# Four plain weight pairs instead of two, and column halves in turn for the products of values and scores, in a kernel of decayed attention and two feed-forward networks

## The chip, the cores and the metric

The kernel runs on one core of one Trainium2 chip. The metric is the device time of one execution in microseconds, here the median of three runs. Five engines matter: PE (TensorE, the matmuls; its weight loads are listed apart as PEld), DVE (VectorE), ACT (ScalarE), POOL (GpSimd) and SP, which here issues the DMAs. Each works its own instructions in the order in which they were written.

## The reference, cut to what matters

The input is q, k, v of shape (2, 8, 768, 64): 2 sequences, 8 heads, 768 tokens, 64 channels.

```python
# attention with decay lam (one number per head), in blocks of 64 tokens
intra = (qb @ kb.T) * Dmask          # Dmask[i, j] = lam ** (i - j) for i >= j, else 0
out   = intra @ vb + (qb * lam_pow) @ kv_state
kv_state = lam ** 64 * kv_state + (kb * rev_pow).T @ vb
# two feed-forward networks, one after the other, on 1536 tokens x 512 channels
h = x @ w_in                         # 512 -> 2048
x = (h * tanh(log1p(exp(h)))) @ w_out            # 2048 -> 512, mish
h = x @ w_in2
y = (h * (1 / (1 + exp(-h)))) @ w_out2           # silu
```

All is in float32 and the result is float32.

## The kernel before, in words

Tokens are worked in chunks of 128 in the attention (12 chunks, 6 for each sequence) and in blocks of 512 in the networks (three blocks, t = 0, 1, 2). A network's 2048 hidden units are 16 tiles n of 128; the second network's tiles go on as n = 16 to 31. Tiles come in pairs p = n // 2, and in groups g of four tiles. NF is 16 and NG, the groups of a network, is 4; so the kernel has groups 0 to 7, and pairs 0 to 15.

**Numbers in two parts.** Matmuls of the networks run on fp32r operands. To keep float32's precision each operand is split into a high part, which ACT casts (xh, wh, gh), and a low part, the rest, which POOL or DVE subtracts (xl, wl, gl). A product is then three matmuls: high x high, low x high, high x low. The weights arrive by DMA in another form (their 64 bits are unpacked on DVE): `split_op` (L122 to L138) is five DVE operations for each half of a tile (half 0 is the part of w_in, half 1 that of w_out), and `run_parts` (L173) has ACT cast wh and POOL subtract wl (L178, L179). In the second network's first group ACT takes over the first of the five (L94) from an item on.

**Two ways to project.** A projection of one tile and one token block, `emit_h` (L407 to L423), is 12 matmuls. For the token blocks 0 and 1, most pairs of tiles are done together by `Block` (L528 on) in seven products of 6 matmuls (m1 to m7) instead of eight, by the scheme of Strassen and Winograd: that needs sums of quarters of x (`sums`, made once for each network by `make_sums` or `evac`), and differences of quarters of w (`sum_pair`, four DVE operations L164 for each pair, two casts, two subtractions). m1's bank "a" is copied to bank "b" by ACT (L568), m5's to `fifth` (L573), and DVE adds that to further banks (L557); m2 goes on adding into bank "a", so it waits for the copy. Pairs in `plain` have no `sum_pair`; they are projected with `emit_h`. Output products, `emit_o` (L425 to L445), are 12 matmuls into four banks `po`, which `evac` (L457) adds to the accumulators at the end of a group: DVE adds (L465), or in a network's group 0 ACT copies (L463). At the end of the first network `evac` also makes the next network's input from the accumulator: xh by ACT (L475), xl by POOL (L478) through the list `rest`, whose entries `run_rest` issues one or more at a time.

**Order.** The order of every engine's work is written by hand. First comes the attention of four chunks, then 12 steps, each with one chunk of attention (while there are any), one projection and one output product of group 0. Then come the groups 1 to 7, each a list of items; after each item `run_parts`, `run_rest`, `run_sums` (sums of x, a list at a time) and `run_split(k)` (k split operations) are called, and the loads of freed slots. Groups 1 and 4 (`first`) begin with four `emit_h` of their first pair in place of seven products, since the sums aren't made yet. The last two, or four, output products of block 2 of a group are the `fills` of the next. In groups 1 and 4 the second pair B (pairs 3 and 9) goes through seven products and the group's output products of t = 0 and 1 stand between B's products and the projections of t = 2.

**The attention's products.** `emit_S` makes the scores (K is 64, a product uses one half of the array's rows, the two heads of a pair in turn), `emit_state` the state (64 columns, the two heads of a pair in turn on the column halves), and `emit_O` (L338) the output of a chunk: four products on state (L344), then for each of eight heads the values times the masked scores (L350), 64 of the array's 128 columns each: all four pairs for the first column half, then all four for the second. DVE multiplies the scores by the mask (L307). Each float32 product shows as two records in the trace.

Of the kernel before, what the change touches and what calls it, by code (L numbers as in the profile page):

```python
# [7 lines left out]
F32 = mybir.dt.float32  # L8
# [9 lines left out]
def decay_attention_mish_silu_kernel(  # L18
# [8 lines left out]
    nc = tc.nc  # L27
    P = 128
# [5 lines left out]
    NP = H // 2  # L34
    T = 512
# [43 lines left out]
    parts = []  # L79

    pre = []
    plain = (2, NF // 2)
    silu = []
    uses = {}

# [252 lines left out]
    def emit_O(n):  # L338
        c = n % CPS
        vn = nat.pop(n)[3]  # L340
        px = ps_a.tile([P, NP, C], F32, tag="a", name="px")
        if c > 0:
            for p in range(NP):
                nc.tensor.matmul(  # L344
                    px[:, p, :], lhsT=states[n % 2][:, p, :], rhs=qd[n][:, p, :],
                    start=(p == 0), stop=False, skip_group_check=True,
                )
        for hh in range(2):
            for p in range(NP):
                nc.tensor.matmul(  # L350
                    px[64 * hh : 64 * hh + 64, p, :], lhsT=vn[:, 2 * p + hh, :], rhs=sm[n][:, hh, p, :],
                    start=(c == 0 and p == 0), stop=(p == NP - 1), skip_group_check=True,
                )
        xslots.append(held.pop(("x", n)))
        xh, xl = x_tile(n // CPB)
        o = slice((n % CPB) * C, (n % CPB + 1) * C)
        xf = wk.tile([P, T], F32, tag="wa", name="xf").rearrange("p (a c) -> p a c", a=NP)
        nc.scalar.copy(xf, px)
        nc.scalar.copy(xh[:, :, o], xf)  # L359

        def finish():
            (nc.vector if n < PH else nc.gpsimd).tensor_tensor(out=xl[:, :, o], in0=xf, in1=xh[:, :, o].bitcast(F32), op=ALU.subtract)

        return finish
# [82 lines left out]
    def cast(i, f):  # L447
        return lambda: nc.scalar.copy(sums[i][0], f)

    def low(i, f):  # L450
        hi, lo = sums[i]
        return lambda: nc.vector.tensor_tensor(out=lo, in0=f, in1=hi.bitcast(F32), op=ALU.subtract)  # L452

    def tt(out, in0, in1, op):
        return lambda: nc.vector.tensor_tensor(out=out, in0=in0, in1=in1, op=op)

    def evac(mm, g, t):  # L457
        if g == 0:
            accs[mm, t] = (accp if t == 0 else late[1]).tile([P, 4, T], F32, tag="acc", name="acc")
        acc = accs[mm, t]  # L460
        for j in range(4):
            if g == 0:
                nc.scalar.copy(acc[:, j, :], po[t][j])  # L463
            else:
                nc.vector.tensor_tensor(out=acc[:, j, :], in0=po[t][j], in1=acc[:, j, :], op=ALU.add)  # L465
            if g == NG - 1 and mm == 1:
                r0 = t * T + j * P
                nc.sync.dma_start(out[r0 : r0 + P, :], acc[:, j, :])
        if g < NG - 1 or mm == 1:
            return  # L470

        xh, xl = x_tile(t)

        def part(j):
            nc.scalar.copy(xh[:, j, :], acc[:, j, :])  # L475
            rest.append((
                (t, j),
                lambda: nc.gpsimd.tensor_tensor(  # L478
                    out=xl[:, j, :], in0=acc[:, j, :], in1=xh[:, j, :].bitcast(F32), op=ALU.subtract
                ),  # L480
            ))

        if t != 1:
            for j in range(4):
                part(j)
            return
        a1, a2 = accs[0, 0], acc

        f1 = late[0].tile([P, 2, T], F32, tag="t4", name="s1", bufs=1)
        f3, f4 = a2[:, 0:2], a1[:, 2:4]  # L490
        add, sub = ALU.add, ALU.subtract
        drain = lambda: run_rest(len(rest))
        summing.extend([
            [tt(f1, a2[:, 0:2], a2[:, 2:4], add)],
            [cast(0, f1), lambda: part(0), lambda: part(1)],
            [low(0, f1), lambda: part(2), lambda: part(3), tt(f1, f1, a1[:, 0:2], sub)],
            [drain, cast(1, f1), tt(f4, f4, f1, sub)],
            [low(1, f1), tt(f3, a1[:, 0:2], f3, sub)],
            [cast(2, f3)],
            [low(2, f3)],  # L500
        ])
        last_sum.append([cast(3, f4), low(3, f4)])
# [5 lines left out]
    def make_sums():  # L508

        x0, x1 = x_tile(0), x_tile(1)  # L510
        sh, sl = [late[0].tile([P, 3, 2, T], F32R, tag=t, name=t, bufs=1) for t in ("sh", "sl")]
        sums.extend((sh[:, i], sl[:, i]) for i in range(3))
        sums.append((x1[0][:, 0:2], x1[1][:, 0:2]))
        q = lambda xt, k: [xt[i][:, 2 * k : 2 * k + 2].bitcast(F32) for i in (0, 1)]
        a11, a12, a21, a22 = q(x0, 0), q(x0, 1), q(x1, 0), q(x1, 1)
        tmp = late[1].tile([P, 4, T], F32, tag="acc", name="tmp")
        f1, f2 = tmp[:, 0:2], tmp[:, 2:4]
        f3 = late[0].tile([P, 2, T], F32, tag="t4", name="s3", bufs=1)
        add, sub = ALU.add, ALU.subtract
        summing.extend([  # L520
            [tt(f1, a21[0], a22[0], add), tt(f1, f1, a21[1], add), tt(f1, f1, a22[1], add), tt(f2, f1, a11[0], sub)],
            [cast(0, f1), tt(f2, f2, a11[1], sub), tt(f3, a11[0], a21[0], sub), tt(f3, f3, a11[1], add), low(0, f1)],
            [cast(1, f2), tt(f1, a12[0], f2, sub), tt(f1, f1, a12[1], add), tt(f3, f3, a21[1], sub), low(1, f2)],
            [cast(2, f3), low(2, f3)],
        ])
        last_sum.append([cast(3, f1), low(3, f1)])

    class Block:  # L528

# [105 lines left out]
    for i, (t, f) in enumerate(steps):  # L635
# [6 lines left out]
            make_sums()  # L642
        if i == len(steps) - 1:
            split_pair(3)
            sum_pair(3)
        for half in halves.get(i, ()):
            split_w(*half)
        if n < N:
# [29 lines left out]
    for g in range(1, 2 * NG):  # L678
        n0 = g * GF
        pa = n0 // 2  # L680
        A, B = Block(pa), Block(pa + 1)
        o = lambda t, f, a=False, b=False: lambda: emit_o(t, n0 + f, a, b)

        os = [(0, 0), (0, 1), (0, 2), (0, 3), (1, 1), (1, 0), (1, 3), (1, 2)]
        if g == 1:
            os = os[4:] + os[:4]
        os = [o(t, f, i % 4 == 0, i % 4 == 3) for i, (t, f) in enumerate(os)]
        hs = [lambda n=n0 + f: emit_h(2, n) for f in range(GF)]
        sp = lambda fn, *a: lambda: fn(*a)
        more = pa + 2 < NF  # L690
        nxt = [[lambda p=p: split_pair(p)] if p < NF else [] for p in (pa + 2, pa + 3)]
        if nxt[0]:
            nxt[0].append(lambda: sum_pair(pa + 2))
        fill = [[fn, sp(split_w, n0 + j, 1)] for j, fn in enumerate(fills + [idle] * (4 - len(fills)))]
        first = g in (1, NG)
        if g > 1:
            fill[0].append(lambda: sum_pair(pa + 1))
        fill[3] += nxt[0]
        if first:

            order = ((1, 1), (1, 0), (0, 0), (0, 1)) if g == 1 else ((0, 0), (0, 1), (1, 1), (1, 0))
            ha = [[lambda t=t, n=n0 + f: emit_h(t, n)] for t, f in order]
            ha[1 if g == 1 else 3].append(lambda: summing.append(last_sum.pop()))
            items = [it for i in range(4) for it in (ha[i], fill[i])]
        else:
            items = [[A.m1], [A.m5], fill[0], [A.m2], [A.m6], fill[1], [A.m7], [A.m3], fill[2], [A.m4], fill[3]]
        items += [
            [B.m1], [B.m5], [B.m2], [B.m6], [os[0]], [B.m7], [B.m3], [os[1]], [B.m4], [os[2]], [os[3]],
            [hs[0]], [os[4]], [hs[1], *nxt[1]], [os[5]], [hs[2]], [os[6]], [hs[3]], [os[7]],
        ]  # L710
        for at, item in enumerate(items):
            if g == NG and at == 7:
                silu.append(True)
            run_later()
            k = len(parts)
            for fn in item:
                fn()
            run_parts(k)
            run_rest(0 if g == NG and 7 <= at < 14 else 1)
            run_sums(1)  # L720
            small = isinstance(getattr(item[0], "__self__", None), Block)
            k = 1 if small else 0 if item[0] is idle else 3 if item[0] in hs or at < (18 if first else 11) else 2
            if g == NG and at < 8:
                k = (0, 1, 1, 1, 1, 3, 3, 3)[at]
            elif g == NG - 1 and at == len(items) - 1:
                k = 0
            run_split(k)
            pump()
        fills = [lambda n=n0 + f: emit_o(2, n, n % GF == 0, n % GF == GF - 1) for f in range(GF)]
# [49 lines left out]
```

## Time and profile before

| | |
|---|---|
| median of 3 runs | 606.63 us (605.3 to 607.45) |
| profiled execution | 607.67 us, its span 605.9 us |
| PE busy | 575.0 us, 2870 matmul records |
| PE weight load busy | 469.3 us |
| DVE busy | 418.2 us, 520 instructions |
| ACT busy | 239.2 us, 439 |
| POOL busy | 325.5 us, 237 |
| mean granted clock of TensorE | 0.979 |

A trace row gives the start in us, the duration, the engine, the line of the kernel, the operation, what it writes and reads, and how many such rows were merged. In brackets stands how long the engine had been idle before it, and what it was released by. Matmuls overlap in the pipeline, so a row's duration is longer than the distance of two starts.

### The profile page before, as it was taken

To read this page: it belongs to the slowest core of one execution; us is meant where nothing else is said; L and a number is where in the kernel's file an instruction comes from. 1 tells how busy PE (TensorE), PEld (TensorE's weight loads), DVE (VectorE), ACT (ScalarE), POOL (GpSimd) and SP (SyncE) were. 2 spreads that over 40 slices of the span, in tenths; PEclk is the share of its full clock that TensorE was granted. 3 is DMA by queue.
4 is the path that set the end of the run, shared out by engine and by line. 5 is a ranking of instruction groups with operands and counts; after the bars stand their busy time and mean duration, and the time that the engine had idled before them with its cause. 6 is when DMAs were issued, how large, how long until landed. Compare 5 with 4: busy or idle time off the path is not lost. (4 is left out here: it accounts for less than half of the span.)

```text
span 605.9 us, 7515 instructions
## 1 busy us (share of the span) xinstructions
PE 575.0 (95%) x2870; PEld 469.3 (77%) x2870; DVE 418.2 (69%) x520; ACT 239.2 (39%) x439; POOL 325.5 (54%) x237
## 2 busy tenths in 40 slices
PE   7899999997899999999999859999999999999997
PEld 4777778886678888888887647788788878888886
DVE  3898963799858687768797779838834895567102
ACT  2435442436413334324426244446433542353220
POOL 1758783346446365646494548737554646445320
PEclk8999999999989999999999879999999999999999
DMA  7955720012322122312221112222402131200103
GB/s 253 421 179 165 288 70 1 1 35 70 104 67 73 36 69 76 98 36 70 70 70 36 35 35 70 69 70 70 133 6 70 46 102 62 70 1 1 70 0 138
DMA packets 14627, 50.55 MB, mean 83 GB/s; under 512 B 1528, under 2 KB 3072, under 8 KB 13312
## 3 DMA queue, kind: packets, MB, share of 16 engines
q1 hardware_dynamic: 14592, 50.08, 24.3%
q8 instruction: 22, 0.36, 0.2%
q14 instruction: 13, 0.11, 0.1%
HBM read 46.92 MB, written 3.15 MB: 83 GB/s over the span
## 5 line engine op out<-in xcount | busy, mean ns | idle before, releaser
L403 POOL TENSOR_TENSOR gl<-wa,gh 128x512 fp32r<-128x512 f32 x96 | 143.8, 1504 | 130.6 <-ACT gh L402 49.1
L179 POOL TENSOR_TENSOR wl<-dec,wh 128x512 fp32r<-128x512 f32 x64 | 88.4, 1381 | 84.9 <-ACT wh L178 84.8
L465 DVE TENSOR_TENSOR acc<-po,acc 128x512 f32<-128x512 f32 x72 | 46.4, 685 | 73.8 <-PE po L441 73.8
L399 ACT ACTIVATE wa<-ph 128x512 f32<-128x512 f32 x48 | 28.8, 599 | 154.2 <-PE ph L418 138.6
L441 PE MATMUL po<-gh,wh 128*128 128x512 f32 x192 | 76.8, 400 | 1.3 <-ACT wh L178 1.3
L418 PE MATMUL ph<-xl,wh 128*128 128x512 f32 x192 | 73.8, 392 | 4.0 <-POOL xl L478 4.0
L441 PE MATMUL po<-gh,wl 128*128 128x512 f32 x192 | 76.1, 396 | 0.9 <-POOL wl L179 0.9
L138 DVE SCALAR_TENSOR_TENSOR dec<-slot,dec 128x512 uint32<-128x512 uint32 x64 | 74.8, 1168 | 1.9
L418 PE MATMUL ph<-xh,wh 128*128 128x512 f32 x192 | 75.7, 394 | 0.2 <-ACT xh L359 0.2
L441 PE MATMUL po<-wl,gh 128*128 128x512 f32 x192 | 74.8, 390 | 0.9 <-POOL wl L179 0.9
L441 PE MATMUL po<-wh,gl 128*128 128x512 f32 x192 | 74.7, 389 | 0.0
L441 PE MATMUL po<-wh,gh 128*128 128x512 f32 x192 | 74.7, 389 | 0.0
L132 DVE TENSOR_SCALAR dec<-dec 128x512 f32<-128x512 f32 x64 | 47.4, 740 | 34.7 <-ACT dec L94 33.6
L136 DVE SCALAR_TENSOR_TENSOR dec<-slot,dec 128x512 uint32<-128x512 uint32 x64 | 60.6, 947 | 2.1
L402 ACT CAST gh<-wa 128x512 fp32r<-128x512 f32 x96 | 58.4, 623 | 1.1
L178 ACT CAST wh<-dec 128x512 fp32r<-128x512 f32 x64 | 39.6, 619 | 44.7 <-DVE dec L138 44.7
L418 PE MATMUL ph<-xh,wl 128*128 128x512 f32 x192 | 53.5, 393 | 0.0
L441 PE MATMUL po<-gl,wh 128*128 128x512 f32 x192 | 51.9, 392 | 0.0
L134 DVE TENSOR_SCALAR dec<-dec 128x512 uint32<-128x512 uint32 x64 | 49.7, 777 | 2.0
L179 POOL TENSOR_TENSOR tl<-t,th 128x512 fp32r<-128x512 f32 x24 | 33.6, 1408 | 24.6 <-ACT th L178 21.0
L418 PEld LDWEIGHTS ph<-xl,wh 128*128 128x128 f32 x192 | 36.0, 188 | 13.0 <-POOL xl L478 5.7
L441 PEld LDWEIGHTS po<-gh,wh 128*128 128x128 f32 x192 | 36.7, 191 | 10.3 <-ACT wh L178 1.7
(106 smaller groups left out, 962.2 us busy)
## 6 DMA issues: line engine op xcount, KB each, us to landing
slot<-w SPq DMA_DIRECT2D x64, 512.0 KB, 3.7
xslot<-x SPq DMA_DIRECT2D x10, 1024.0 KB, 9.0
out<-acc SPq DMA_DIRECT2D x12, 256.0 KB, 2.1
xslot<-x SPq DMA_DIRECT2D x4, 512.0 KB, 4.4
dmask<-scr SPq DMA_DIRECT2D x2, 256.0 KB, 4.5
lamrow<-scr SPq DMA_DIRECT2D x2, 128.0 KB, 6.7
pw<-lam SPq DMA_DIRECT2D x1, 0.0 KB
scr<-pw SPq DMA_DIRECT2D x1, 8.0 KB
```

The lines of the kernel that those rows point to most:

```text
L132: nc.vector.tensor_scalar(out=df, in0=df, scalar1=2.0**-15, scalar2=None, op0=ALU.max)
L134: nc.vector.tensor_scalar(out=d, in0=d, scalar1=3, scalar2=0x3FFFFFF8, op0=shl, op1=band)
L136: nc.vector.scalar_tensor_tensor(out=d, in0=low, scalar=29, in1=d, op0=shr, op1=bor)
L138: nc.vector.scalar_tensor_tensor(out=d, in0=high, scalar=0xC0000000, in1=d, op0=band, op1=bor)
L178: nc.scalar.copy(hi, f)
L179: nc.gpsimd.tensor_tensor(out=lo, in0=f, in1=hi.bitcast(F32), op=ALU.subtract)
L399: nc.scalar.activation(a, ps, AF.Mish if mm == 0 else AF.Silu)
L402: nc.scalar.copy(gh, a)
L403: nc.gpsimd.tensor_tensor(out=gl, in0=a, in1=gh.bitcast(F32), op=ALU.subtract)
L418: nc.tensor.matmul(ph, lhsT=wi[wsel][:, kk * P : (kk + 1) * P], rhs=xt[xsel][:, kk, :], start=(i == 0), stop=(i == 3 * KD - 1),)
L441: nc.tensor.matmul(po[t][j], lhsT=lhsT, rhs=rhs, start=(first and wsel + gsel == 0), stop=(last and gsel == 1))
L465: nc.vector.tensor_tensor(out=acc[:, j, :], in0=po[t][j], in1=acc[:, j, :], op=ALU.add)
```

## The change

Two edits. In `emit_O` the loops over pairs and column halves change places, so that products of the two column halves alternate. And the pairs 3 and 9 join 2 and 8 as plain pairs: groups 1 and 4 now consist of eight `emit_h` (t = 0, four tiles, with the late output products between them; then t = 1, with t = 0's output products between them), then the projections of t = 2 and t = 1's output products. With it, in `make_sums` the fourth sum's additions move to after the last projection of group 1, into a buffer of their own; in `evac` the casts of block 1 no longer alternate with the sums but precede them; `sum_pair` of the group after moves behind the first projection of t = 2; and the counts of split operations per item change in groups 1 and 4.

```diff
-    plain = (2, NF // 2)
+    plain = (2, 3, NF // 2, NF // 2 + 1)
@@ emit_O
-        for hh in range(2):
-            for p in range(NP):
+        for p in range(NP):
+            for hh in range(2):
                 nc.tensor.matmul(
                     px[64 * hh : 64 * hh + 64, p, :], lhsT=vn[:, 2 * p + hh, :], rhs=sm[n][:, hh, p, :],
@@ evac
-        def part(j):
+        for j in range(4):
             nc.scalar.copy(xh[:, j, :], acc[:, j, :])
             rest.append((
...
         if t != 1:
-            for j in range(4):
-                part(j)
             return
...
         summing.extend([
+            [], [drain],
             [tt(f1, a2[:, 0:2], a2[:, 2:4], add)],
-            [cast(0, f1), lambda: part(0), lambda: part(1)],
-            [low(0, f1), lambda: part(2), lambda: part(3), tt(f1, f1, a1[:, 0:2], sub)],
-            [drain, cast(1, f1), tt(f4, f4, f1, sub)],
+            [cast(0, f1)],
+            [low(0, f1), tt(f1, f1, a1[:, 0:2], sub)],
+            [cast(1, f1), tt(f4, f4, f1, sub)],
@@ make_sums
-            [cast(1, f2), tt(f1, a12[0], f2, sub), tt(f1, f1, a12[1], add), tt(f3, f3, a21[1], sub), low(1, f2)],
+            [cast(1, f2), tt(f3, f3, a21[1], sub), low(1, f2)],
...
-        last_sum.append([cast(3, f1), low(3, f1)])
+        def fourth():
+            f4 = late[0].tile([P, 2, T], F32, tag="t4", name="s4", bufs=1)
+            h2, l2 = (s.bitcast(F32) for s in sums[1])
+            for fn in (tt(f4, a12[0], h2, sub), tt(f4, f4, a12[1], add), tt(f4, f4, l2, sub)):
+                fn()
+            summing.append([cast(3, f4), low(3, f4)])
+        last_sum.append([fourth])
@@ groups
+        first = g in (1, NG)
+        os = [(0, 0), (0, 1), (0, 2), (0, 3)] + [(1, f) for f in (range(4) if first else (1, 0, 3, 2))]
...
-            ha = [[lambda t=t, n=n0 + f: emit_h(t, n)] for t, f in order]
-            ha[1 if g == 1 else 3].append(lambda: summing.append(last_sum.pop()))
-            items = [it for i in range(4) for it in (ha[i], fill[i])]
+            hp = [[lambda t=t, n=n0 + f: emit_h(t, n)] for t in range(2) for f in range(GF)]
+            hp[-1].append(lambda: summing.append(last_sum.pop()))
+            items = [it for i in range(4) for it in (hp[i], fill[i])]
+            items += [it for i in range(4) for it in (hp[4 + i], [os[i]])]
+            items.append([hs[0], lambda: sum_pair(pa + 2)])
...
-            run_rest(0 if g == NG and 7 <= at < 14 else 1)
+            run_rest(0 if g == NG and 7 <= at < 12 else 1)
...
-            k = 1 if small else 0 if item[0] is idle else 3 if item[0] in hs or at < (18 if first else 11) else 2
+            k = 1 if small else 0 if item[0] is idle else 3 if item[0] in hs or at < (8 if first else 11) else 2
             if g == NG and at < 8:
-                k = (0, 1, 1, 1, 1, 3, 3, 3)[at]
+                k = (1, 1, 1, 2, 2, 2, 2, 2)[at]
```

## Rows read from the trace of the kernel before

**Rows 1.** The page's busy table: us, share of the span, instructions.
```profile
PE 575.0 (95%) x2870; PEld 469.3 (77%) x2870; DVE 418.2 (69%) x520; ACT 239.2 (39%) x439; POOL 325.5 (54%) x237
```

**Rows 2.** The chain of waits, stage 2: start, us, what, how many.
```profile
353.46 0.61 DVE acc L465
...
354.10 1.82 ACT xh L475 x4
...
358.15 0.49 ACT b L568
...
358.69 2.93 PE a L549 x6
...
379.96 1.44 POOL xl L478
...
391.03 2.72 PE ph L418 x12
```

**Rows 3.** The table of stages: stretch, length, busy us of each engine, granted clock.
```profile
127.76:195.80 68.04, 62.55 (x260) 50.54 (x258) 54.32 (x67) 25.66 (x46) 37.65 (x26) 0.95 0.24 78
320.92:401.91 80.99, 69.14 (x284) 54.93 (x283) 62.27 (x61) 37.06 (x63) 51.37 (x34) 0.94 0.17 56
```

**Rows 4.** PE's waits over the span: for whom, total us, times, longest.
```profile
PE a L549 <- ACT b L568: 10.8, 3, 7.0
PE ph L418 <- POOL xl L478: 4.0, 4, 1.5
...
PE po L441 <- POOL wl L179: 1.7, 2, 0.9
...
PE pc L326 <- DVE sm L307: 1.1, 1, 1.1
```

**Rows 5.** The timeline of ACT, then of PE, in stage 1.
```profile
148.00 0.62 ACT L178 CAST wh<-dec 128x512 fp32r<-128x512 f32 x1 [3.44 <-DVE dec L138]
...
150.30 1.07 PE L549 MATMUL a<-xh,wh 128*128 128x512 f32 x2 [3.35 <-ACT b L568]
```

**Rows 6.** Split operations: groups over the span (mean ns of one), then DVE's timeline.
```profile
L138 DVE SCALAR_TENSOR_TENSOR dec<-slot,dec 128x512 uint32<-128x512 uint32 x64 | 74.8, 1168 | 1.9
...
L130 DVE TENSOR_SCALAR dec<-slot 128x512 uint32<-128x512 uint32 x39 | 29.3, 751 | 0.0
...
128.51 1.52 DVE L130 TENSOR_SCALAR dec<-slot 128x512 uint32<-128x512 uint32 x1
...
304.31 1.52 DVE L130 TENSOR_SCALAR dec<-slot 128x512 uint32<-128x512 uint32 x1
...
310.43 1.66 DVE L138 SCALAR_TENSOR_TENSOR dec<-slot,dec 128x512 uint32<-128x512 uint32 x1
```

**Rows 7.** DVE's timeline in stage 2: two additions of the sums.
```profile
322.95 1.23 DVE L455 TENSOR_TENSOR s<-acc 128x1024 f32<-128x1024 f32 x1
...
330.58 2.31 DVE L455 TENSOR_TENSOR acc<-acc,s 128x1024 f32<-128x1024 f32 x1
```

**Rows 8.** POOL's groups over the span: count, busy us, mean ns of one.
```profile
L403 POOL TENSOR_TENSOR gl<-wa,gh 128x512 fp32r<-128x512 f32 x96 | 143.8, 1504 | 130.6 <-ACT gh L402 49.1 <-PE b L549 41.1 <-issue 30.6
L179 POOL TENSOR_TENSOR wl<-dec,wh 128x512 fp32r<-128x512 f32 x64 | 88.4, 1381 | 84.9 <-ACT wh L178 84.8
...
L478 POOL TENSOR_TENSOR xl<-acc,xh 128x512 fp32r<-128x512 f32 x12 | 20.1, 1689 | 0.0
```

**Rows 9.** PE's timeline around the products of one attention chunk.
```profile
58.69 0.69 PE L326 MATMUL pc<-xslot,kd 128*64 128x64 f32 x16
59.30 1.16 PE L344 MATMUL px<-qd,state 128*128 128x128 f32 x8
60.39 1.58 PE L350 MATMUL px<-sm,xslot 128*64 128x128 f32 x16
61.90 0.50 PE L441 MATMUL po<-gh,wh 128*128 128x512 f32 x1
...
64.85 1.16 PE L305 MATMUL s<-xslot 64*128 64x128 f32 x16
65.94 0.50 PE L418 MATMUL ph<-xh,wh 128*128 128x512 f32 x1
```

**Rows 10.** DVE's timeline in the attention: the score masks of four chunks.
```profile
46.85 1.29 DVE L307 TENSOR_TENSOR sm<-s,dmask 128x512 f32<-128x512 f32 x2 [1.27 <-PE s L305]
...
57.82 1.29 DVE L307 TENSOR_TENSOR sm<-s,dmask 128x512 f32<-128x512 f32 x2
...
69.32 1.29 DVE L307 TENSOR_TENSOR sm<-s,dmask 128x512 f32<-128x512 f32 x2
...
87.68 1.29 DVE L307 TENSOR_TENSOR sm<-s,dmask 128x512 f32<-128x512 f32 x2 [3.23 <-PE s L305]
```

More of the change, by code (lines that the diff above doesn't have):

```diff
@@ L477, in part @@
                 (t, j),
-                lambda: nc.gpsimd.tensor_tensor(
+                lambda j=j: nc.gpsimd.tensor_tensor(
                     out=xl[:, j, :], in0=acc[:, j, :], in1=xh[:, j, :].bitcast(F32), op=ALU.subtract
@@ L644, in decay_attention_mish_silu_kernel @@
             split_pair(3)
-            sum_pair(3)
         for half in halves.get(i, ()):
@@ L682, in decay_attention_mish_silu_kernel @@
         o = lambda t, f, a=False, b=False: lambda: emit_o(t, n0 + f, a, b)
-        os = [(0, 0), (0, 1), (0, 2), (0, 3), (1, 1), (1, 0), (1, 3), (1, 2)]
-        if g == 1:
-            os = os[4:] + os[:4]
+        first = g in (1, NG)
+        os = [(0, 0), (0, 1), (0, 2), (0, 3)] + [(1, f) for f in (range(4) if first else (1, 0, 3, 2))]
         os = [o(t, f, i % 4 == 0, i % 4 == 3) for i, (t, f) in enumerate(os)]
@@ L691, in decay_attention_mish_silu_kernel @@
         nxt = [[lambda p=p: split_pair(p)] if p < NF else [] for p in (pa + 2, pa + 3)]
-        if nxt[0]:
+        if nxt[0] and not first:
             nxt[0].append(lambda: sum_pair(pa + 2))
         fill = [[fn, sp(split_w, n0 + j, 1)] for j, fn in enumerate(fills + [idle] * (4 - len(fills)))]
-        first = g in (1, NG)
-        if g > 1:
+        if not first:
             fill[0].append(lambda: sum_pair(pa + 1))
@@ L699, in decay_attention_mish_silu_kernel @@
         if first:
-            order = ((1, 1), (1, 0), (0, 0), (0, 1)) if g == 1 else ((0, 0), (0, 1), (1, 1), (1, 0))
-            ha = [[lambda t=t, n=n0 + f: emit_h(t, n)] for t, f in order]
-            ha[1 if g == 1 else 3].append(lambda: summing.append(last_sum.pop()))
-            items = [it for i in range(4) for it in (ha[i], fill[i])]
+            hp = [[lambda t=t, n=n0 + f: emit_h(t, n)] for t in range(2) for f in range(GF)]
[3 more added lines that the diff above has]
+            items.append([hs[0], lambda: sum_pair(pa + 2)])
         else:
             items = [[A.m1], [A.m5], fill[0], [A.m2], [A.m6], fill[1], [A.m7], [A.m3], fill[2], [A.m4], fill[3]]
[L707 to L710, printed above, removed]
+            items += [
+                [B.m1], [B.m5], [B.m2], [B.m6], [os[0]], [B.m7], [B.m3], [os[1]], [B.m4], [os[2]], [os[3]], [hs[0]],
+            ]
+        items += [[os[4]], [hs[1], *nxt[1]], [os[5]], [hs[2]], [os[6]], [hs[3]], [os[7]]]
         for at, item in enumerate(items):
```

## The prediction

> **What bounds the kernel now.** I read the busy table first: PE is busy 95% of the span [rows 1]. The reader is to see that no other engine can be the bound on average, so the time is the number of matmuls times their pitch, plus the stretches in which PE does not hold that pitch. The chain of waits gives the pitch: twelve 512-column matmuls, one projection, start 2.72 us before the next [rows 2], 0.2267 us each. The table of stages then shows where the pitch fails [rows 3]. Stage 1 is group 1 of the first network (127.76 to 195.80 us): by the code it issues 258 matmuls (4 projections of 12, 2 late output products of 12, 42 of the pair done by seven products, 8 output products and 4 projections of 12), worth 58.5 us, and takes 68.04. So 9.55 us are lost. Stage 2 is group 4, the first of the second network, 320.92 us to about the first product of the next group at 401.91: 282 matmuls, 63.9 us, but 80.99: 17.1 us lost. The list of PE's waits names the cause [rows 4]: 10.8 us in three waits for ACT's copy "b" (L568), 7.0 us the longest, and 4.0 us for POOL's xl (L478). The granted clock of the two stages is 0.95 and 0.94 [rows 3]: part of the loss is matmuls at 1.2 GHz after a wait.
>
> The timeline shows how the copy comes late [rows 5]. In stage 1 PE has issued m1 and m5 and waits 3.35 us for ACT's copy; ACT, in order, had stood 3.44 us at the cast of a weight half whose DVE split was late. In stage 2 the chain runs over DVE's accumulators, the four xh casts L475 that wait for them, then the copy [rows 2]. Both are the same thing: a seven-product pair gives PE only the 6 matmuls of m5 (1.4 us) before it needs ACT back, while DVE and ACT are full of sums and splits.
>
> **The change, part by part.**
>
> *Four plain pairs instead of two.* In groups 1 and 4 the second pair also becomes plain: 48 matmuls for 42, twice, so +12 x 0.2267 = +2.72 us on PE, unhidden. What goes: both stages' copies L568/L573 and adds L557, pair 3's and pair 9's input differences (8 DVE subtractions, 4 ACT casts, 4 POOL subtractions), all beside PE. Projections now come in the order t=0 (four), t=1 (four), t=1's output products and t=2 after; each needs ACT only four banks later, so it has 10.9 us of cover instead of 1.4. If all lost time went, the two stages would take 264 and 288 matmuls, 59.85 and 65.3 us, against 68.04 and 80.99: 23.9 us less.
>
> *What is late next in stage 1.* Weight halves: DVE's split of a half is five operations whose means add to 4.4 us [rows 6] (the first and the last of the five lines stand there). Two additions of the fourth sum leave the late attention (some 2 to 4.6 us less DVE work there) and one more buffer keeps the third token block's accumulators from waiting for the sums. DVE then comes to the first half at about 124 us, where today it is 128.5 [rows 6], has six halves to deliver before the fourth output product (26 us), two more and the fourth sum's three additions (1.23 to 2.31 each, [rows 7]) before 165 us: 35 + 5.5 = 41 us of work in 41 us. Tight, but the list is served ahead: the second half (due 19 us after group 1 starts) would be ready 10 us before that, the later ones 5 us or more. Left over: 0 to 4 us; I take 0.5 us, near zero for that lead.
>
> *What is late next in stage 2.* (a) The sums now wait until after the casts of xh, and POOL's four xl are issued at once; block t=1 is wanted only from 320.92 + 8 x 2.72 = 342.7 us, where today it is 320.92 + 4 x 2.72 = 331.8. That wait goes. (b) DVE: from 322.9 [rows 7] to the end of the last late product (342.7) stand two splits (8.8 us) and six additions (7.4 to 13.9 us), then the accumulators of t=2, which must free their banks for the first output product at 345.4 us. DVE is through at 339 to 346 by these, later since the second operation waits for an ACT cast behind the second projection (329.1 us, with the activation and the cast about 331). The worst: with a half at the 7.8 us that one took under POOL's load [rows 6] it is 353 us, a wait of 8. I take 0.5 us. (c) POOL: the xl of t=2 are held back until item 12 and issued one per item to item 15; the projection of t=2 at item 16 reads the fourth at its eighth matmul, 364.4 + 1.6 = 366 us. From about 357.5 us (the seventh projection's end at 356.3, its activation and a weight's cast on ACT) POOL has two weight halves, two gl and four xl in front of that, 2 x 1.38 + 2 x 1.50 + 4 x 1.69 = 12.5 us [rows 8], so 370 us: 4 us late. With xl at the 1.44 us that the chain has for one [rows 2] it is 3.0, with a stretch at half clock behind it 5.5. I take 4.0 us. So 5.0 us remain of the 26.65 (range 0.5 to 13, where not all comes to its worst at once).
>
> *Values times scores in alternating column halves.* 12 chunks of 8 products, two records each. Now a chunk takes 61.90 - 60.39 = 1.51 us, 94 ns a record [rows 9]. The neighbours tell what alternating does: the score products alternate row halves and take 65.94 - 64.85 = 1.09 us for 16 records, 68 ns, and the state products alternate column halves: 0.61 us, 38 ns (half the columns). The full-array products take 1.09 us for 8, 136 ns. If a record is weight load plus stream, 136 and 94 ns give 42 ns per 64 weights and 53 ns per 128 columns. Two alternating halves side by side would give 68 for the scores (it is 68) and 34 for the state products (it is 38). For this line: 47 ns, 0.75 us a chunk, at most 0.76 us saved, 9.1 us over twelve; nothing saved is the other end. A loss I exclude: the shapes and loads are the same. I take 0.72 us. Not every chunk keeps it, since DVE's score masks are due soon after: at 57.82 and 69.32 us the mask starts without DVE having idled, and PE waits 1.1 us for one; at 46.85 and 87.68 us DVE itself idled for PE [rows 4, 10]. So chunks 1 to 4, 6 and 7 lose their gain to DVE's chain, and 0, 5 and 8 to 11 keep it: 6 x 0.72 = 4.3 us.
>
> The Trainium skill speaks against this edit: "TensorE: Matmul & The Clock Gate", Part 3, says that weight loads overlap running matmuls only when the row group differs, so by it column halves would gain little. The state products disagree: serial load and stream would be 69 ns a record, and it is 38. By the page's rule the sum would be 4.3 us higher.
>
> *The sum.* The profiled execution took 607.67 us, 605.9 of it span. 607.67 - 26.65 + 2.72 + 5.0 - 4.3 = 584.4; the median of the three runs is 1.04 lower, 606.63, so 583.4 us.
>
> **Rivals.**
> 1. *A DVE wait takes the place of the ACT wait.* In stage 2 the first output product waits for t=2's accumulators behind sums and splits: 8 us by the worst case above, some 1.6 at half clock, while POOL's lateness at (c) goes, since POOL has that time to catch up: 606.63 - 23.9 + 0.5 + 9.6 - 4.3 = 588.5. For it: DVE is busy 62 of 81 us there and 54 of 68 in stage 1 [rows 3]. Against: in both, most of DVE's list can run ahead of PE.
> 2. *Column halves gain nothing.* 583.4 + 4.3 = 587.7. For it: serial today. Against: the 38 ns.
> 3. *All goes as far as it can.* 606.63 - 23.9 + 0.5 - 9.1 = 574.1. Against: (c), and DVE's chain at 47 to 84 us.
> 4. *Slower.* DVE becomes the bound of stage 1. With plain pairs PE wants its weights 8 us sooner while nine halves, a pair's differences, the fourth sum and eight accumulators remain. At 4.4 us a half this is some 40 + 3 + 7 + 5 = 55 us, under 59.85. At 7.8 us a half it is 70 + 3 + 9 + 5 = 87 us, 19 more than the stage has now; stage 2 in the same way would keep its 81: 606.63 + 19 - 4.3 = 621. It decides from a mean half of 5.9 us (54 + 15 = 68). Against: the mean of the whole run is 4.4.
>
> **How the numbers follow.** Chances: forecast 0.60, rival 1 0.15, rival 2 0.10, rival 3 0.10, rival 4 0.05. The range 576.5 to 592.5 takes in the unknowns of the likeliest (remaining waits 0.5 to 13, columns 0 to 9.1, not all at one end), both rivals at 588, and leaves out rival 3's far end and rival 4. A measurement here can tell about 0.3% (1.8 us). Faster: the first four cases less a little, 0.93; within 0.3%: 0.02; slower: 0.05.
>
> **What would show it.** In the changed profile: no wait for L568 at all in groups 1 and 4, and the first seven-product pair 59.9 us after the start of group 1, 65 to 72 us in group 4; the px products of a chunk 0.75 to 0.85 us apart from what follows; a PE wait "ph <- POOL xl" before the first t=2 projection of group 4, and perhaps "po <- DVE acc" before its first output product. The attention part should end 4 us earlier, at about 102 us instead of 105.95. The prediction is wrong if a wait for DVE of over 5 us stands in either stage, or if px keeps 1.5 us a chunk.

## The result, and the profile after

The changed kernel takes 588.75 us (median of four runs, 587.66 to 589.93), the kernel before, run beside it, 607.04: a ratio of 0.970 with a 95% interval of 0.9666 to 0.9734, 18 us faster. That is inside the range of 576.5 to 592.5 and 5.4 us above the forecast of 583.4. The profiled execution took 588.31 us, 586.5 of it span.

The busy table of the changed kernel: PE has 8 us less busy time [rows 1] and the span is 19.4 us shorter.

```profile
span 586.5 us, 7516 instructions
...
PE 567.0 (97%) x2882; PEld 463.6 (79%) x2882; DVE 409.0 (70%) x509; ACT 235.7 (40%) x431; POOL 318.6 (54%) x233
```

The table of stages of the changed kernel (columns as in rows 3; the first stretch is group 1, the second group 4):

```profile
126.73:187.09 60.36, 60.36 (x265) 49.24 (x265) 58.78 (x65) 23.34 (x41) 34.25 (x24) 1.00 0.24 79
312.21:383.42 71.21, 67.28 (x288) 54.87 (x288) 51.38 (x55) 35.06 (x59) 45.45 (x31) 0.98 0.19 63
```

The stretches of this table and the end of stage 2 in [rows 3] come from the chain of waits, which can stand 0.16 us behind PE's own rows. By the starts of PE's rows, group 1 fell from 68.04 us (127.76 to 195.80) to 60.36 (126.57 to 186.93), group 4 from 80.83 (320.92 to 401.75) to 71.37 (312.05 to 383.42). Between them stand the same 125.12 us in both kernels. Group 1 starts only 1.19 us earlier, and the part after group 4 is 1.07 us shorter. So 7.7 + 9.5 + 1.2 + 1.1, with the rounding 19.4 us. The last term is hardly the change's: from the second pair of group 6 to group 7 it takes 43.2 us in the kernel before and 42.2 in this profile, but 43.1 to 43.4 in six of the nine other runs below and 42.2 in three.

PE's waits in the changed kernel (for whom: total us, times, longest):

```profile
PE ph L418 <- POOL xl L478: 3.9, 2, 2.4
PE pc L326 <- ACT kd L289: 3.6, 2, 1.9
PE px L350 <- DVE sm L307: 3.6, 4, 1.9
...
PE pc L326 <- DVE sm L307: 1.4, 1, 1.4
...
PE a L555 <- ACT b L574: 0.4, 1, 0.4
```

In group 1 its weight loads wait four times for DVE's accumulators:

```profile
PEld po L441 <- DVE acc L465: 1.1, 4, 0.3
```

Of the 10.8 us for ACT's copy [rows 4] 0.4 is left, outside both stages. In group 1 PE is busy throughout, with the clock at 1.00. What is left in group 4 stands in one place, the first projection of block 2. PE's timeline there, then POOL's:

```profile
358.44 0.50 PE L418 MATMUL ph<-xl,wh 128*128 128x512 f32 x1 [1.58 <-POOL xl L478]
...
361.53 0.50 PE L418 MATMUL ph<-xl,wh 128*128 128x512 f32 x1 [2.35 <-POOL xl L478]
361.86 1.77 PE L418 MATMUL ph<-xh,wl 128*128 128x512 f32 x4
363.43 0.63 PE L441 MATMUL po<-wh,gh 128*128 128x512 f32 x1
```

```profile
353.63 1.29 POOL L478 TENSOR_TENSOR xl<-acc,xh 128x512 fp32r<-128x512 f32 x1
354.89 1.29 POOL L179 TENSOR_TENSOR wl<-dec,wh 128x512 fp32r<-128x512 f32 x1
356.14 2.24 POOL L478 TENSOR_TENSOR xl<-acc,xh 128x512 fp32r<-128x512 f32 x1
358.35 1.45 POOL L403 TENSOR_TENSOR gl<-wa,gh 128x512 fp32r<-128x512 f32 x1
359.76 1.71 POOL L478 TENSOR_TENSOR xl<-acc,xh 128x512 fp32r<-128x512 f32 x1
```

The third and the fourth xl hold up PE, each behind another subtraction of POOL. After the waits (3.93 us) the next matmuls start 0.43 us apart instead of 0.23: the granted clock from 361.53 to 365.50 us was 0.57, so most of that ran at 1.2 GHz. From 355.57, where this projection starts, to 367.10, where the next but one item does, pass 11.53 us, where two items want 5.44: 6.1 us.

The products of values and scores, a chunk where nothing waits and one where DVE's masks are late:

```profile
38.88 1.09 PE L350 MATMUL px<-sm,xslot 128*64 128x128 f32 x16
39.91 1.16 PE L305 MATMUL s<-xslot 64*128 64x128 f32 x16
...
23.56 0.43 PE L350 MATMUL px<-sm,xslot 128*64 128x128 f32 x2 [1.33 <-DVE sm L307]
24.16 1.09 PE L350 MATMUL px<-sm,xslot 128*64 128x128 f32 x14 [0.16 <-DVE sm L307]
25.18 1.16 PE L305 MATMUL s<-xslot 64*128 64x128 f32 x16
```

The first chunk takes 39.91 - 38.88 = 1.03 us (64 ns a record) instead of 1.51 [rows 9]: 0.48 us saved, not 0.72. These two rows show how many records PE starts in the first 0.41 us of a chunk, in the kernel before (60.39 to 60.80 us) and in the changed one (38.88 to 39.29):

```profile
60.39 0.65 PE L350 MATMUL px<-sm,xslot 128*64 128x128 f32 x4
38.88 0.66 PE L350 MATMUL px<-sm,xslot 128*64 128x128 f32 x8
```

The starts of the single records in the trace say more. In a block on one half a record starts every 109 ns. With the halves in turn two records start 6 to 7 ns apart, and the next two 109 ns after them. So the two halves run side by side, each at the pitch that it has alone. The weight load is not what is saved: the records on state (L344), with twice the weights, start 112 ns apart, hardly more than 109, and those with 64 moving columns (L326) start in pairs 58 ns apart, so a record's time goes with its moving columns. The kernel before had part of this already: the second half's first record starts at 60.885 us, 0.49 us after the first half's, and ahead of the first half's last three (60.989, 61.098 and 61.207 us). The trace doesn't name the half of a record; it is read from the pitch. So the 94 ns of [rows 9] are a mean over records alone and records side by side.

The second chunk shown above takes 25.18 - 23.56 = 1.62 us, and that is what such a chunk took before. This is PE's timeline of the kernel before for chunk 3:

```profile
28.91 1.69 PE L350 MATMUL px<-sm,xslot 128*64 128x128 f32 x16 [2.12 <-DVE sm L307]
30.53 1.16 PE L305 MATMUL s<-xslot 64*128 64x128 f32 x16
```

Alternating, the third record already needs the second half of the mask, which DVE makes 0.6 us after the first; before, four products of the first half stood between. Where the mask is late, a shorter series gains nothing.

### The profile page after: what moved, and what is told of

Read it like the earlier page. It is cut to its first block, busy times and chain, and to the rows that moved or that the text cites. A ratio compares the mean times of both kernels' runs of the same rounds, so it can differ in the third digit from the quotient of the medians.

```text
span 586.5 us, 7516 instructions
## 1 busy us (share of the span) xinstructions
PE 567.0 (97%) x2882; PEld 463.6 (79%) x2882; DVE 409.0 (70%) x509; ACT 235.7 (40%) x431; POOL 318.6 (54%) x233
## 4 chain that ended last, share of the span: by engine, by line
PE 85%; DVE 8%; DMA 2%; ACT 2%; issue 1%; POOL 1%; SPq 0%; ACTq 0%; POOLq 0%
PE po L441 43%; PE ph L418 24%; PE b L555 7%; PE a L555 4%; PE c L555 2%; PE e L555 2%; DVE sm L307 1%; DVE dec L132 1%; DVE dec L130 1%; DVE dec L136 1%; DMA dmask<-scr 1%; PE px L350 1%; DVE dec L134 1%; DVE dec L138 1%; PE px L344 1%
## 5 line engine op out<-in xcount | busy, mean ns | idle before, releaser
L403 POOL TENSOR_TENSOR gl<-wa,gh 128x512 fp32r<-128x512 f32 x96 | 141.6, 1480 | 116.8 <-PE b L555 40.3
L399 ACT ACTIVATE wa<-ph 128x512 f32<-128x512 f32 x56 | 33.5, 599 | 158.7 <-PE ph L418 154.7
L418 PE MATMUL ph<-xl,wh 128*128 128x512 f32 x224 | 86.0, 390 | 3.9 <-POOL xl L478 3.9
L418 PE MATMUL ph<-xh,wh 128*128 128x512 f32 x224 | 88.2, 394 | 0.0
L132 DVE TENSOR_SCALAR dec<-dec 128x512 f32<-128x512 f32 x64 | 49.5, 774 | 40.8 <-ACT dec L94 39.7
L138 DVE SCALAR_TENSOR_TENSOR dec<-slot,dec 128x512 uint32<-128x512 uint32 x64 | 66.8, 1044 | 1.9
L418 PE MATMUL ph<-xh,wl 128*128 128x512 f32 x224 | 62.1, 393 | 0.0
L136 DVE SCALAR_TENSOR_TENSOR dec<-slot,dec 128x512 uint32<-128x512 uint32 x64 | 60.4, 944 | 2.1
L418 PEld LDWEIGHTS ph<-xl,wh 128*128 128x128 f32 x224 | 42.1, 188 | 13.3 <-POOL xl L478 4.8
L418 PEld LDWEIGHTS ph<-xh,wh 128*128 128x128 f32 x224 | 42.1, 188 | 9.6 <-issue 0.2
L418 PEld LDWEIGHTS ph<-xh,wl 128*128 128x128 f32 x224 | 42.3, 189 | 8.8
```

What stands on the lines that cost most here:

```text
L132: nc.vector.tensor_scalar(out=df, in0=df, scalar1=2.0**-15, scalar2=None, op0=ALU.max)
L136: nc.vector.scalar_tensor_tensor(out=d, in0=low, scalar=29, in1=d, op0=shr, op1=bor)
L138: nc.vector.scalar_tensor_tensor(out=d, in0=high, scalar=0xC0000000, in1=d, op0=band, op1=bor)
L403: nc.gpsimd.tensor_tensor(out=gl, in0=a, in1=gh.bitcast(F32), op=ALU.subtract)
L418: nc.tensor.matmul(ph, lhsT=wi[wsel][:, kk * P : (kk + 1) * P], rhs=xt[xsel][:, kk, :], start=(i == 0), stop=(i == 3 * KD - 1),)
```

## The experiments

### Each of the two edits alone

One kernel is the kernel before with this edit alone, the other the changed kernel with this edit undone:

```diff
-        for hh in range(2):
-            for p in range(NP):
+        for p in range(NP):
+            for hh in range(2):
```

> The kernel before with the alternating column halves alone. In the changed kernel a chunk's products of values and scores take 1.03 us instead of 1.51, so 0.48 us x 12 = 5.8 us could be saved. Theory (DVE's chain of masks and weight splits sets the pace of most chunks, so most of it turns into waits of PE for DVE): 1 to 2.5 us faster than before, about 605.3 us, px again 1.03 us a chunk, waits 'px <- DVE sm' and 'pc <- DVE sm' longer than the 3.2 us of before. Rival (all of it counts, and the changed kernel's profile merely started late behind the DMA of dmask): 5 to 6 us faster, about 601.5 us.

Measured: 605.22 us, ratio 0.9963 to the kernel before (0.9946 to 0.9981): 2.2 us faster, with an interval of 1 to 3. PE's waits of this kernel, and below them one of the kernel before that [rows 4] leaves out:

```profile
PE a L549 <- ACT b L568: 10.8, 3, 7.0
PE ph L418 <- POOL xl L478: 4.0, 4, 1.5
PE px L350 <- DVE sm L307: 3.7, 3, 2.6
PE pc L326 <- DVE sm L307: 2.0, 2, 1.4
```

```profile
PE px L350 <- DVE sm L307: 2.1, 1, 2.1
```

The waits of groups 1 and 4 are those of [rows 4] to the tenth; those for the masks grew from 3.2 to 5.7 us. The theory's number holds.

> The changed kernel with the old order of column halves, so the plain groups alone. Theory (DVE's chain absorbs the column gain): 1 to 2.5 us slower than the changed kernel, 590 to 591 us, with the first seven-product pair of group 2 again about 60.4 us after the start of group 1. Rival (columns worth 5 to 6 us): about 594 us.

Measured: 590.56 us, ratio 0.9731 (0.9700 to 0.9762) to the kernel before, 1.8 us slower than the changed kernel. The first seven-product pair of group 2 starts 60.40 us after group 1, as the theory has it. So the plain groups bring some 16.5 us, the columns about 2, and within the intervals the two add up. The 1.8 us alone are not clear of noise, since the intervals of the two ratios overlap (0.9666 to 0.9734 and 0.9700 to 0.9762); the 2.2 us of the run before are. What the moves made with the plain pairs (the fourth sum, the casts in `evac`, the split counts) bring by themselves wasn't tried. (The kernel before had a median of 607.04 us beside the changed kernel, and of 607.76 and 608.12 beside the experiments. By the ratios, each to its own, the differences from the changed kernel that follow shift by up to 1.3 us.)

### POOL's queue in group 4

```diff
-            run_rest(0 if g == NG and 7 <= at < 12 else 1)
+            run_rest(0 if g == NG and at == 7 else 1)
```

> The changed kernel, in which the four xl subtractions of token block 2 in group 4 are issued from item 8 on instead of item 12 (same work, earlier place in POOL's queue). Theory (the 6.1 us that group 4 still loses is POOL's queue alone: 3.9 us of waits for xl and the half clock behind them): no wait 'ph <- POOL xl', 5 to 6 us faster than the changed kernel, about 583 us. Rival (POOL is short of time in this stage, so that weight halves or gl come late in place of xl): 0 to 2 us, with a new wait 'po <- POOL wl' in items 9 to 13.

Measured: 583.31 us (582.97 to 583.7), ratio 0.9615 (0.9588 to 0.9642): 5.4 us faster than the changed kernel. From the first product a of group 2 to that of group 5 pass 192.17 us instead of 196.49: 4.3 us are won in this stretch. Where the rest of the 5.4 comes from isn't shown; the two profiles differ by as much in parts that the edit doesn't touch (group 1 starts at 125.27 us here, at 126.57 in the changed kernel). PE's waits behind 100 us:

```profile
PE po L441 <- ACT acc L463: 1.0, 1, 1.0
PE b L555 <- DVE c L563: 0.6, 1, 0.6
PE a L555 <- ACT b L574: 0.5, 1, 0.5
PE po L441 <- POOL wl L179: 0.2, 1, 0.2
```

No wait for xl is left; a weight half costs 0.2 us and the accumulators of block 0, which ACT copies only after the fourth sum has been read, 1.0 us. POOL was idle for some of the time between items 8 and 12, and the order alone had cost 4.3 of the 6.1 us.

### Less work, or more cover?

```diff
-    plain = (2, 3, NF // 2, NF // 2 + 1)
+    plain = (2, NF // 2)
...
             split_pair(3)
+            sum_pair(3)
...
+        if g == NG:
+            fill[3].append(lambda: sum_pair(pa + 1))
         fill[3] += nxt[0]
```

> The changed kernel, in which the differences of pairs 3 and 9 are made all the same, on DVE, ACT and POOL (8 subtractions, 4 casts, 4 subtractions), and not used; the projections stay plain. Pair 9's come at item 7 of group 4. Theory (the plain groups help because PE no longer waits for ACT soon after a product, not because the other engines have less to do): 0 to 2 us slower than the changed kernel, 589 to 591 us, and no wait for ACT's copy in groups 1 and 4. Rival (less work on DVE and POOL is what helps): 6 us slower or more, 595 us and up.

Measured: 595.51 us (595.34 to 596.2), 6.8 us slower than the changed kernel. The number is the rival's. But no wait for ACT's copy came back, as the theory has it. PE's timeline of this kernel in group 1 shows late weight halves, and the four DVE operations stand in front of these in DVE's list (134.44 to 138.19 us):

```profile
145.88 0.50 PE L441 MATMUL po<-gh,wl 128*128 128x512 f32 x1 [0.84 <-POOL wl L179]
...
163.80 0.49 PE L441 MATMUL po<-gh,wh 128*128 128x512 f32 x1 [1.25 <-ACT wh L178]
...
165.15 0.50 PE L441 MATMUL po<-gh,wl 128*128 128x512 f32 x1 [0.86 <-POOL wl L179]
```

From the start of the last chunk's px to group 2 it takes 91.27 us (the changed kernel 86.00), from there to group 5 200.17 (196.49), and PE's waits for xl in group 4 grew from 3.9 us to 5.7. To tell the amount of work from its place, the same was issued later:

```diff
-    plain = (2, 3, NF // 2, NF // 2 + 1)
+    plain = (2, NF // 2)
...
-            items.append([hs[0], lambda: sum_pair(pa + 2)])
+            items.append([hs[0], lambda: sum_pair(pa + 1), lambda: sum_pair(pa + 2)])
```

> The differences of pairs 3 and 9 in vain once more, the same work as in the run that took 595.5 us, but issued at item 16 of groups 1 and 4, behind the weight halves of the group's output products. Theory (what cost 6.8 us there was the place in DVE's queue, in front of the halves, and POOL's queue in front of xl): 589 to 590.5 us. Rival (the amount of work costs it, wherever it stands): 594 us or more.

Measured: 590.20 us (589.29 to 591.27), ratio 0.9712 (0.9690 to 0.9735), 1.45 us slower than the changed kernel (0.7 by the ratios, whose intervals overlap). The two stretches take 86.02 and 198.46 us: nothing is lost in group 1, and 2.0 us in the second. They stand in group 2, just behind group 1, where PE waits for the accumulators, which DVE starts at 189.28 us here and at 186.45 in the changed kernel:

```profile
190.02 0.50 PE L441 MATMUL po<-gh,wh 128*128 128x512 f32 x1 [1.20 <-DVE acc L465]
```

From the first product a of group 2's second pair to group 5 it takes 176.1 us in both. So it is mostly the place in DVE's and POOL's queues, and little the amount. The theory is right in that the waits for ACT's copy, 10.8 us, went with the plain pairs and not with the smaller amount of work. It left out DVE's list: in front of the weight halves of group 1 these differences cost 5.3 us (91.27 against 86.00), behind them nothing there.

### What swallows the column gain

```diff
-        run_split((6, 3, 4, 4, 4, 4, 4, 4, 4, 0, 0, 0)[i])
+        run_split((6, 3, 4, 3, 3, 3, 3, 4, 4, 0, 0, 0)[i])
...
-        run_split((2, 0, 4, 4, 4, 4, 4, 4, 0, 0, 0, 5)[i])
+        run_split((2, 0, 4, 2, 2, 2, 2, 4, 0, 0, 0, 5)[i])
```

> The changed kernel, in which the split operations of attention steps 3 to 5 (8, 8, 4) are spread over steps 3 to 6 (5 each), so that DVE stands less in front of the score masks of chunks 8 and 9; all else as it was. Theory (DVE's chain in front of the masks is what swallows the column gain): the wait 'pc <- DVE sm' of 1.4 us at about 70 us goes and the attention ends 1.5 to 3 us earlier, 586 to 587 us. Rival (the chunks are held by the start, by the DMA of dmask and x, or by POOL): within 0.5 us of the changed kernel.

Measured: 586.70 us (585.58 to 586.96), 2.05 us faster than the changed kernel. PE's waits from 34 to 106 us in the changed kernel, and in this one:

```profile
PE pc L326 <- DVE sm L307: 1.4, 1, 1.4
PE px L344 <- POOL qd L294: 0.4, 1, 0.4
```

```profile
PE px L344 <- POOL qd L294: 0.3, 1, 0.3
```

> The same spread of split operations, with the old order of column halves. Theory: with DVE less in the way more of the 5.8 us of column gain arrives, so this one is 2.5 to 4 us slower than the kernel with the spread and the alternating halves (without the spread the difference was 1.8 us). Rival: the difference stays at 1.8 us or falls.

Measured: 590.22 us (588.82 to 591.07): 3.5 us slower than the same with alternating halves. The number is the theory's, but that the spread doubles the gain isn't shown, since the 1.8 us without it are not clear of noise. In the profiles the last px of the attention starts 2.5 us earlier with the halves in turn and the spread (99.20 us against 101.66). Without the spread it is 1.7 us in the kernel with that edit alone (101.27 against 102.94), 1.5 to 1.8 in the three other runs with the changed kernel's attention (100.45 to 100.74 against 102.22), and 0.5 in the changed kernel's own profile (101.75), whose masks came late. So DVE's chain takes part of the gain, but most of the 5.8 us is missing in both. The waits for masks before 34 us don't tell the orders apart: 2.7 us with the halves in turn, 2.8 in blocks. The clock does in part. From 28 to 36 us the granted clock is 1.00 in all three profiles with the halves in blocks. It is 0.79 in six of the eight with changing halves, and there the fifth chunk's px start at 37.3 to 38.9 us, where in blocks they start at 35.9 to 36.6. What lowers it isn't shown.

### Both mends

> The changed kernel with both mends: xl of block 2 from item 8 of group 4, and the spread of split operations in the attention. The two touch different stages, so the gains should add: 583.3 less what the spread gives alone, 581 to 582 us. If the spread gives nothing: 583.3.

Measured: 582.58 us (580.87 to 583.96), ratio 0.9580 (0.9554 to 0.9605). It beats both kernels, the changed one by 6.2 us. Against the kernel with the early xl alone it is 0.7 us better in the median, with overlapping runs; that the spread's 2 us add in full isn't shown.

### What a change of the column half does

```diff
-        for p in range(NP):
-            for hh in range(2):
+        for hh, p in [(hh, q + p) for q in (0, 2) for hh in range(2) for p in range(2)]:
+            if True:
```

> The changed kernel, in which the column half changes after every second product of values and scores (0, 0, 1, 1, 0, 0, 1, 1) instead of after each: 4 of a chunk's 8 products follow one on the other half, 4 one on the same half. Theory (a change of the half hides a product's weight load, nothing else; streams still go one after the other): half of the 0.48 us is lost, a chunk takes about 1.27 us. Rival (the half matters only within a chunk's order of banks or pairs, or once for the chunk): 1.03 us as with full alternation, or 1.5 us as before.

Measured, in one run: 588.57 us. PE's timeline of a chunk, and how many records start in its first 0.41 us (81.22 to 81.63):

```profile
81.23 1.15 PE L350 MATMUL px<-sm,xslot 128*64 128x128 f32 x16
82.30 0.50 PE L441 MATMUL po<-gh,wh 128*128 128x512 f32 x1
```

```profile
81.23 0.67 PE L350 MATMUL px<-sm,xslot 128*64 128x128 f32 x8
```

A chunk takes 1.07 us, 67 ns a record: nearly all of the saving with fewer than half of the changes (3 instead of 7). The theory that each change hides one weight load falls, and so does the rival's part of 1.5 us. The theory's other half, that streams follow one another, falls too: eight records start in 0.41 us, as with full alternation. The single starts show why. The other half's first record starts 14 ns after the chunk's first, past three records that stand before it in the program, and from there the halves run side by side. In blocks of four products it also goes past three records, but only after five have started: that is the 0.49 us. So in these traces PE takes a record of the other half past three that haven't started, and the statement at the front, that each engine works in the written order, doesn't hold between the halves. Rows of different lines in the kernel before show it too, a px record ahead of a pc record that the program has before it:

```profile
12.77 0.42 PE L350 MATMUL px<-sm,xslot 128*64 128x128 f32 x1
12.87 0.31 PE L326 MATMUL pc<-xslot,kd 128*64 128x64 f32 x1
```

Whether three is the limit wasn't tried with other lengths.

## Why the prediction was right, and where it was off

- **What bounds the kernel.** Right: the lost time stood in the two stages, and 17.1 of the 19.4 us were won there. The part between them didn't change by a hundredth.
- **12 matmuls more, the waits for ACT's copy gone.** Right: 59.85 + 0.5 = 60.35 us forecast for group 1, 60.36 measured. That it fits to the hundredth is luck, since the 0.5 us were meant for late weight halves and no such wait came; in their place stand the four waits for DVE's accumulators, at one output product (167.37 us on). The reason was incomplete: the run with the differences in vain shows that they also had to leave the front of DVE's queue. The prediction listed them among the work "beside PE" and gave them no price.
- **Group 4, (a) and (b).** Right. Neither block 1's xl nor the accumulators of block 2 hold up PE; DVE started the latter at 335.27 us, 1.3 us before the first output product. The stage starts 8.9 us earlier now, so that is 344.1 us on the clock of before, inside the 339 to 346 of the prediction.
- **Group 4, (c).** The place and the queue were right, the size not: 4.0 us forecast, 6.1 measured. The wait alone is 3.93 us; the step left the half clock behind it, which stood in the upper bound of 5.5, out of the value taken. The mended order wins 4.3 us in this stretch.
- **Column halves.** This is the step that failed in size: 4.3 us forecast, 2.2 (1 to 3) and 1.8 measured. The mechanism, two halves side by side, was right. Two terms were wrong. The first is the saving of a chunk, 0.48 us and not 0.72: the prediction took 94 ns for a record alone and halved it, but alone it takes 109, and a chunk's ends (0.16 us from the first start to the next on a half, 0.2 from the last start to the next product) stay as they are. That makes 0.48 x 6 = 2.9 us. Its split of a record into weight load and stream doesn't hold either (112 ns with twice the weights). The second term is which chunks keep their gain. A late chunk saves nothing, since it now wants the second mask earlier (1.62 us before and after); DVE's chain takes a part; and in six of eight profiles the granted clock from 28 to 36 us is 0.79. The sign for the attention failed with it: the first projection behind it was to start 4 us earlier, and starts at 104.81 us instead of 106.00.
- **The Trainium skill's rule.** The Trainium skill, "TensorE: Matmul & The Clock Gate", Part 3, has weight loads overlap only where the row group differs. The prediction took from it that alternating column halves would gain little. The trace disagrees with that: eight records start in 0.41 us with the halves in turn, four in blocks.
- **The sum.** 23.2 us forecast, 18.3 measured. In the two profiles, which differ by 19.4, the attention brings 1.2 us where 4.3 were forecast, group 1 the 7.7 that were, group 4 9.5 instead of 11.2 (6.1 us stayed lost, not 4.5), and the part behind it 1.1 that nothing forecast. In the profiled run the first masks' DMA also landed late: ACT's second group of kd operations starts at 12.85 us, in the kernel before at 11.40, in others of these profiles from 10.71 on. The three other runs with the same attention code start group 1 at 125.27 to 125.56 us instead of 126.57, so about 1 us of the attention's shortfall in this profile is that.
- **Rivals.** No wait of PE for DVE came in stage 2 (rival 1), the columns gained something (rival 2), the waits for xl and the columns kept the time well above 574.1 us (rival 3), and DVE did not become group 1's bound (rival 4), though it was busy 58.8 of 60.4 us there: four more operations in the wrong place brought waits at once.

## What to carry to other kernels

Count, for each product, how long PE can go on before it needs another engine's answer, and compare it with what stands in that engine's queue: six more matmuls were cheap against a copy that came 3 to 7 us late. When a stage has become dense, the place of an operation in an in-order queue weighs more than its length: the same sixteen small operations cost 6.8 us in one place and about 1 in another, and four subtractions moved forward won 4.3 us in their stretch. A saving on PE in a stage where another engine sets part of the pace arrives only in part: of the 5.8 us that the column halves save on PE, about 2 did.

## What was not expected of the hardware

- Products on the two halves of the array's columns run side by side, each half at its own 109 ns a record. It is almost enough that the half changes after two products (67 ns a record in the mean of a chunk) instead of after each (64 ns), against 94 ns when it changes after four: PE goes past three records that haven't started.
- After 3.93 us of waits within 5 us, nine matmuls started some 0.4 us apart, at a granted clock of 0.57, then all at 0.23 again.
